# Keeping the source's order for eight more steps of a chunked recurrence with a feed-forward layer

## The chip, the core and the metric

One core of one Trainium2 chip. The metric is the device time of one execution in microseconds (us); times are compared as medians over runs. The engines named here are TensorE (PE, matrix products), VectorE (DVE), ScalarE (ACT), GpSimd (POOL) and SyncE (SP, which only issues DMAs here).

## What is computed

A gated linear recurrence over 4 batches of 8 heads of 768 positions, in chunks of 32, and behind it a feed-forward layer on its 3072 output rows of 256 values. Cut to what matters:

```python
for c in range(nc):                                   # 24 chunks of 32 positions
    L = np.exp(cum[:, :, :, None] - cum[:, :, None, :]) * causal
    M = np.einsum('bhin,bhjn->bhij', Cc, Bc) * L
    y_intra = np.einsum('bhij,bhjd->bhid', M, xc)
    y_inter = np.einsum('bhin,bhnd->bhid', Cc, state) * decay_to_i[:, :, :, None]
    y[:, :, sl] = y_intra + y_inter
    state = decay_full[:, :, None, None] * state + np.sum(Bx, axis=2)
h = y_rows @ w_in                                     # 256 -> 2048
g = np.maximum(h, 0.0) + np.log1p(np.exp(-np.abs(h))) # softplus
out = g @ w_out                                       # 2048 -> 256
```

## The kernel before

**Tiles.** The 768 positions are cut into six tiles u = 0 to 5 of 128 positions; with the four batches a tile holds 512 tokens. "Third tile" is u = 2, "fourth tile" u = 3. For each tile the recurrence makes a 256 x 512 input of the feed-forward layer, and this passes through 16 blocks k of 128 hidden units each.

**Words.** The source issues its work in words, one function each. For a tile u (and half p): `D` writes decays into `rm` (POOL, `affine_select`), `S` makes scores in PSUM (`sp`, PE), `M` multiplies these into `rm` (DVE), `B` scales B into `bp` and `C` scales C into `cc` (DVE), `T` scales the state into `td` (DVE), `U` (PE, `zp`), `I` and `R` (PE, `yp`) are products, `N` makes the next state `tb` (DVE), `G` multiplies `yp` into `gg` (DVE), `Xh` and `Xl` split the result into two parts `xh` (ACT) and `xl` (DVE). For a block k of tile j: `F` is the first product into `hp` (6 matmuls), `P` has three parts, `e` (softplus, ACT), `gh` (rounded copy, ACT, four buffers) and `gl` (the rest, DVE), and `Z` is the second product into `acc` (6 matmuls, which read `gh`, `gl`, `gh`, and again for the other half of the outputs).

**Order.** `ORDER` (lines 58 to 77) is a list of words written out by hand; it covers tiles 0, 1 and 2 of the recurrence and most blocks of the first two tiles. Its end, on which the case turns, is

```python
U2 P1.11 I2.1 R2 E0 G2.0 Z1.8 G2.1 N2 Z1.9 P1.11 P1.11 Xh2.0 Xl2.0 P1.12 P1.13 P1.13 Z1.10 Z1.11 Xh2.1 P1.12 P1.12
P1.15 P1.15 Xl2.1 P1.15
```

Behind it a loop runs over steps s from 32 (line 793). Step s issues Z of the block four steps back, then F and P of its own block, then the words that `FILLS` puts at this step. Steps 32 to 35 issue Z1.12 to Z1.15 and, at 35, `finish(1)`, which adds the sums of the second tile into `o` (two DVE operations) and stores them. Steps 32 to 47 hold F and P of the third tile's blocks 0 to 15; from step 36 their Z follow. For the fourth tile, `FILLS` gives: step 32, `D3.0` and loads for the next tile; step 37, `S3.0`, four `M3.0`, `D3.1`; step 39, `C3` (two operations), `B3.0`, `B3.1`, `T3`; step 40, `S3.1`, four `M3.1`; step 43, `U3 I3 R3 G3 Xh3 Xl3 N3`. The fifth and sixth tile have the same words 16 and 32 steps later.

**What sets the order on an engine.** PE and the DMA queue of SP are always kept in the source's order. DVE, ACT and POOL go through `InOrder` (lines 124 to 132): while `in_order[0]` is true each instruction is pinned behind everything that the source has issued on its engine before. From step `PINNED` on (lines 794 and 795) the flag is false, and the compiler's scheduler may place an instruction of these engines earlier than the source has it, wherever its inputs and buffers are ready in the scheduler's own simulation. The profile tells the two apart: a pinned instruction carries the wrapper's line, L131 (a load L140), a free one the line of its own function, as L400 for `B`, L410 for `C`, L438 for `T`, L396 for `M`, L356 for `D`, L611, L614 and L617 for the parts of `P`.

**Buffers that matter.** `bp` has two, `cc` and `td` one each, so the fourth tile's can be written once `U2`, `R2` and `N2` have read the third tile's. PSUM has six shared banks (`sp`, `hp`, `zp`, `yp`, `fp`) and two accumulators `acc`.

Of the kernel before, what the change touches and what calls it, by code (L numbers as in the profile page):

```python
# [76 lines left out]
"""  # L77
HALF = NFT // 2
AHEAD = 32
PINNED = 34  # L80
LAG = 4
WRAW = 4
END = 4
# [27 lines left out]
def recurrence_then_ffn(ctx: ExitStack, tc: tile.TileContext, un, alr, w_in, w_out, const, outT):  # L111
# [681 lines left out]
    for s in range(AHEAD, len(steps) + LAG):  # L793
        if s == PINNED:
            in_order[0] = False
# [54 lines left out]
```

## Time and profile before

| what | value |
|---|---|
| median of 3 runs | 319.69 us (318.64 to 319.97) |
| the profiled execution | 319.56 us |
| its span, first to last instruction | 317.9 us |
| PE busy | 307.7 us (97%) |
| ACT busy | 169.0 us (53%) |
| DVE busy | 160.9 us (51%) |
| POOL busy | 38.7 us (12%) |
| mean granted clock of TensorE | 0.995 |

Read it so: the profiled execution takes 1.66 us more than its span, and lies 0.13 us below the median. A granted clock of 1.00 is full speed (2.4 GHz), 0.50 the lower level (1.2 GHz). In the timelines an "x2" behind a row is a run of two instructions merged, and the brackets at its end are the idle time of the engine before it and what ended that.

### The profile page before, as it was taken

What the parts mean: (1) busy time and instruction counts of PE and PEld (TensorE: products, weight loads), DVE (VectorE), ACT (ScalarE), POOL (GpSimd) and SP (SyncE); (2) the same over time, 40 slices, a digit from 0 to 9 for tenths busy, and PEclk for the clock granted to TensorE, in tenths of its full rate; (3) what the DMA queues carried; (4) which work ended last, traced back from release to release, by engine and by line L of the source; (5) the groups of instructions that cost most, each with busy time, mean ns of one, the idle gap of its engine ahead of it and who ended that gap; (6) DMA issues with size and microseconds to landing.
All of it is one profiled execution on the core that took longest, in us unless ns stands there. A gap on an engine that the chain in (4) does not pass through costs nothing.

```text
span 317.9 us, 5610 instructions
## 1 busy us (share of the span) xinstructions
PE 307.7 (97%) x2308; PEld 252.9 (80%) x2308; DVE 160.9 (51%) x254; ACT 169.0 (53%) x290; POOL 38.7 (12%) x47
## 2 busy tenths in 40 slices
PE   4999999999999979999999999999999999999995
PEld 4877888888888858888888788888888888888885
DVE  3999995545544863345842345462354242322222
ACT  5799899696835244433344543444533444544450
POOL 5770800000000600000600000420000000000000
PEclk9999999999999979999999999999999999999999
DMA  7957947404000531100430100000100000100001
GB/s 225 405 219 222 381 161 198 134 0 165 2 0 0 193 108 35 64 3 0 150 117 2 66 2 0 3 0 2 66 1 2 3 0 0 64 4 0 2 0 66
DMA packets 10298, 24.37 MB, mean 77 GB/s; under 512 B 1056, under 2 KB 1696, under 8 KB 10272
## 3 DMA queue, kind: packets, MB, share of 16 engines
q1 hardware_dynamic: 10272, 24.01, 22.0%
q8 instruction: 18, 0.29, 0.4%
q14 instruction: 8, 0.07, 0.1%
HBM read 20.76 MB, written 3.24 MB: 76 GB/s over the span
## 4 chain that ended last, share of the span: by engine, by line
PE 92%; DVE 5%; DMA 1%; issue 1%; ACT 1%; DVEq 0%; ACTq 0%
PE acc L131 40%; PE hp L131 40%; PE sp L131 4%; PE yp L131 4%; DVE bp L400 1%; PE fp L131 1%; PE end L131 1%; DMA both_logs<-in_alr 1%; PE zp L131 1%; DVE rm L131 1%; DVE gg L131 0%; DVE wil L131 0%; DVE w L131 0%; PE gp L131 0%; DVE half L131 0%
## 5 line engine op out<-in xcount | busy, mean ns | idle before, releaser
L617 DVE TENSOR_TENSOR gl<-e,gh 128x512 fp32r<-128x512 f32 x62 | 42.9, 691 | 100.1 <-ACT gh L614 100.1
L611 ACT ACTIVATE e<-hp 128x512 f32<-128x512 f32 x62 | 37.1, 598 | 90.5 <-PE hp L131 90.1
L131 PE MATMUL hp<-xh,wih 128*128 128x512 f32 (+1 forms) x196 | 76.2, 389 | 0.5 <-DVE rm L131 0.5
L131 PE MATMUL acc<-gl,woh 128*128 128x512 f32 x188 | 74.1, 394 | 1.9 <-DVE gl L131 1.9
L131 PE MATMUL hp<-xl,wih 128*128 128x512 f32 (+1 forms) x196 | 75.5, 385 | 0.0
L131 PE MATMUL hp<-xh,wil 128*128 128x512 f32 (+1 forms) x196 | 75.5, 385 | 0.0
L131 PE MATMUL acc<-gh,woh 128*128 128x512 f32 x188 | 74.9, 398 | 0.0
L131 PE MATMUL acc<-gh,wol 128*128 128x512 f32 x188 | 73.9, 393 | 0.0
L131 PEld LDWEIGHTS hp<-xh,wih 128*128 128x128 f32 x196 | 37.0, 189 | 8.6 <-DVE rm L131 1.0
L131 PEld LDWEIGHTS acc<-gl,woh 128*128 128x128 f32 x188 | 35.5, 189 | 9.8 <-DVE gl L131 2.7
L131 PEld LDWEIGHTS hp<-xh,wil 128*128 128x128 f32 x196 | 36.8, 188 | 7.7 <-DVE wil L131 0.3
L131 PEld LDWEIGHTS hp<-xl,wih 128*128 128x128 f32 x196 | 36.9, 188 | 7.3
L131 PEld LDWEIGHTS acc<-gh,woh 128*128 128x128 f32 x188 | 35.6, 189 | 8.7 <-issue 0.9
L131 PEld LDWEIGHTS acc<-gh,wol 128*128 128x128 f32 x188 | 35.7, 190 | 7.4
L614 ACT CAST gh<-e 128x512 fp32r<-128x512 f32 x62 | 38.5, 621 | 5.1 <-PE acc L131 3.3
L131 DVE TENSOR_TENSOR gl<-e,gh 128x512 fp32r<-128x512 f32 x34 | 22.9, 688 | 22.1 <-ACT gh L131 22.1
L131 POOL TENSOR_SCALAR_AFFINE_SELECT rm<-fc 128x512 f32<-128x512 f32 (+1 forms) x25 | 22.9, 949 | 80.0 <-PE yp L131 76.2
L131 ACT CAST gh<-e 128x512 fp32r<-128x512 f32 x34 | 20.4, 617 | 10.8 <-PE acc L131 10.6
L131 ACT ACTIVATE e<-hp 128x512 f32<-128x512 f32 x34 | 19.7, 592 | 10.8 <-PE hp L131 7.2
L131 ACT ACTIVATE signs<-wraw 128x512 f16<-128x512 f32 (+1 forms) x32 | 24.2, 783 | 0.0
L356 POOL TENSOR_SCALAR_AFFINE_SELECT rm<-fc 128x2048 f32<-128x2048 f32 x5 | 13.0, 2624 | 87.9 <-PE yp L131 87.9
L131 DVE TENSOR_TENSOR rm<-sp,rm 128x512 f32<-128x512 f32 x24 | 15.5, 683 | 6.9 <-PE sp L131 6.6
(91 smaller groups left out, 222.5 us busy)
## 6 DMA issues: line engine op xcount, KB each, us to landing
un<-in_un SPq DMA_DIRECT2D x10, 768.0 KB, 6.2
wraw<-in_w_in SPq DMA_DIRECT2D x8, 512.0 KB, 5.4
wraw<-in_w_out SPq DMA_DIRECT2D x8, 512.0 KB, 4.3
gg<-gd SPq DMA_DIRECT2D x20, 128.0 KB, 3.4
out_t<-o SPq DMA_DIRECT2D x9, 256.0 KB, 2.1
head_in_h<-in_un SPq DMA_DIRECT2D x2, 384.0 KB, 5.1
head_in_l<-in_un SPq DMA_DIRECT2D x2, 384.0 KB, 6.6
out_t<-half SPq DMA_DIRECT2D x2, 256.0 KB, 2.2
```

What stands on the lines that cost most here:

```text
L131: return lambda *a, **k: tc.keep_in_program_order(f(*a, **k))
L356: Pl.affine_select(out=weights_of(u, p)[:, ks].rearrange("p h (c i) -> p (h c) i", i=SUB), in_=fs.rearrange("p h c -> p (h c)").unsqueeze( ...
L400: V.tensor_tensor(bp, home(u, p)[:, U_B:].rearrange("p (h n) -> p h n", n=N), f_tok[u][0][:, p * KP : (p + 1) * KP].unsqueeze(2).broadcast ...
L611: A.activation(e, h, AF.Softplus)
L614: A.copy(gh, e)
L617: V.tensor_tensor(gl, e, gh.bitcast(F32), op=ALU.subtract)
```

## The change

One constant is raised by eight.

```diff
 HALF = NFT // 2
 AHEAD = 32
-PINNED = 34
+PINNED = 42
 LAG = 4
```

So DVE, ACT and POOL keep the source's order through steps 34 to 41 as well; what the source issues from step 42 on stays free. Of the instructions in these eight steps, those on DVE are the `gl` of the third tile's blocks 2 to 9, `finish(1)`, `M3.0`, `C3`, `B3.0`, `B3.1`, `T3` and `M3.1`; those on ACT are the `e` and `gh` of the same blocks; the one on POOL is `D3.1`. No instruction is added, removed or resized.

## Rows read from the trace of the kernel before

**Rows 1.** Waits of PE, whole span: us in total, times, longest us

```profile
PE fp L131 <- ACT both_logs L131: 4.2, 1, 4.2
PE acc L131 <- DVE gl L131: 1.9, 1, 1.9
PE hp L131 <- DVE rm L131: 0.5, 1, 0.5
PE yp L131 <- DVE rm L131: 0.3, 1, 0.3
```

**Rows 2.** Windows, PE: length, busy time (instructions), granted clock, DMA share, GB/s

```profile
111.66:113.61 1.95, 0.00 (x1) 1.00 0.53 215
113.61:114.42 0.81, 0.81 (x4) 1.00 0.00 0
114.42:117.75 3.33, 3.33 (x9) 0.51 0.19 51
119.21:310.00 190.79, 190.79 (x1307) 1.00 0.07 24
```

**Rows 3.** Timeline of PE: start us, us, engine, line, operation, out<-in

```profile
106.03 1.10 PE L131 MATMUL yp<-cc,tb 32*64 32x128 f32 x32
...
108.33 0.39 PE L131 MATMUL acc<-gh,wol 128*128 128x512 f32 x1
...
109.69 0.39 PE L131 MATMUL acc<-gh,wol 128*128 128x512 f32 x1
...
111.05 0.39 PE L131 MATMUL acc<-gh,wol 128*128 128x512 f32 x1
111.27 0.39 PE L131 MATMUL acc<-gh,woh 128*128 128x512 f32 x1
...
117.75 0.47 PE L131 MATMUL hp<-xh,wih 128*128 128x512 f32 x1
...
128.73 0.39 PE L131 MATMUL acc<-gh,woh 128*128 128x512 f32 x1
```

**Rows 4.** Chain that ended last, in time: start us, us, what

```profile
106.40 3.83 DVE bp L400 x2
...
151.94 0.58 PE zp L131 x32
152.53 2.78 PE yp L131 x96
```

**Rows 5.** Timeline of DVE around the stall

```profile
107.64 2.59 DVE L400 TENSOR_TENSOR bp<-un,ft 128x256 f32<-128x256 f32 x1
...
112.88 0.68 DVE L131 TENSOR_TENSOR gl<-e,gh 128x512 fp32r<-128x512 f32 x1
...
125.53 1.37 DVE L681 TENSOR_TENSOR o<-acc,half 128x512 f32<-128x512 f32 x2 [1.43 <-PE acc L131]
```

**Rows 6.** Timeline of ACT

```profile
108.81 0.62 ACT L131 CAST gh<-e 128x512 fp32r<-128x512 f32 x1 [3.83 <-PE acc L131]
...
125.48 0.62 ACT L614 CAST gh<-e 128x512 fp32r<-128x512 f32 x1
```

**Rows 7.** Timeline of POOL

```profile
107.42 2.56 POOL L356 TENSOR_SCALAR_AFFINE_SELECT rm<-fc 128x2048 f32<-128x2048 f32 x1
153.55 5.47 POOL L356 TENSOR_SCALAR_AFFINE_SELECT rm<-fc 128x2048 f32<-128x2048 f32 x2 [43.58 <-PE yp L131]
```

**Rows 8.** Timeline of DVE later in the span

```profile
143.77 0.69 DVE L617 TENSOR_TENSOR gl<-e,gh 128x512 fp32r<-128x512 f32 x1 [2.02 <-ACT gh L614]
144.38 2.48 DVE L396 TENSOR_TENSOR rm<-sp,rm 128x512 f32<-128x512 f32 x4
...
153.23 0.41 DVE L400 TENSOR_TENSOR bp<-un,ft 128x256 f32<-128x256 f32 x1
...
154.16 2.60 DVE L438 TENSOR_TENSOR td<-tb,fr 128x256 f32<-128x256 f32 x1
156.69 1.27 DVE L517 TENSOR_TENSOR gg<-yp,gg 128x512 f32<-128x512 f32 x2
```

## Prediction

> **What bounds the kernel now.** I read the waits of PE first, because PE is busy for 307.7 of 317.9 us. There are four [rows 1]: 4.2 us at the start for the input, 0.5 and 0.3 for `rm`, and 1.9 us, once, for a `gl`. Only the last lies in the region that the change touches. The windows show where: PE does nothing from 111.66 to 113.61, runs at full clock for 0.81 us more, then 3.33 us at a granted clock of 0.51, the lower of the two levels; from 119.21 to 310 it is busy without a gap, at 1.00 [rows 2]. Two things follow. The stall costs more than its 1.95 us, since a slow stretch comes behind it. And whatever is won there goes straight to the end, because behind it PE never waits again until its last matmuls.
>
> The timeline of PE gives the whole loss. From the last matmul of Z1.8, at 108.33, to the last of Z1.9, at 109.69, are six, so one takes 1.36 / 6 = 0.227 us. Z1.11 begins at 111.27, and F2.0, which comes after twelve matmuls (Z1.11 and Z1.12), at 117.75 [rows 3]: 6.48 us where 12 x 0.227 = 2.72 would do. **3.76 us** are lost: 1.95 idle, 3.33 x (1 - 0.51) = 1.63 to the clock, and 0.18 where the pipe empties and fills.
>
> Why was that `gl` late? The chain of waits leads from `bp`, 3.83 us for two instructions of L400 [rows 4], to the `gl` of P1.11 at 112.88 [rows 5]. These are B3.0 and B3.1: words of step 39, free, which the scheduler has moved ahead of G2.0 at the end of the hand-written list. Behind them on DVE came `G2`, `N2`, and, also moved ahead, C3 and T3, and only then that `gl`. Its input was there much earlier: `gh` of P1.11 runs from 108.81 to 109.43 [rows 6].
>
> **The change part by part.**
>
> *The five operations leave.* All five words lie in steps 34 to 41, so they now stay behind what the source has ahead of them. DVE then goes on after `E0` with G2.0, which needs R2: 106.03 + 1.10 = 107.13 [rows 3]. The pair `gg` takes 1.27 [rows 8], to 108.4. For the two `tb` I take 0.41 each, the `bp` of [rows 8] with twice their columns: to 109.2. `gh` of P1.11 stays where it is, because it waits for the buffer that Z1.8 frees at 108.33 + 0.39 = 108.72 [rows 3, 6]. So its `gl` starts at 109.45 and is done at 110.14. The other bound: D3.1 holds POOL until 107.42 + 2.56 = 109.98 [rows 7], and beside it a `bp` that takes 0.41 alone took 2.59 and ended 0.25 us behind D3.1 [rows 5, 8]. If this `gl` has to wait out D3.1 as well, it ends at 109.98 + 0.69 = 110.67. PE wants it for the second matmul of Z1.11, at 111.27 + 0.23 = 111.50. Both bounds are early enough; this stall is gone.
>
> *What is late next.* Z1.12. Its `gh` needs the buffer that Z1.10 frees at 111.05 + 0.39 = 111.44; starting 0.09 later, as P1.11's did, it ends at 112.15; the `gl` runs from 112.18 to 112.87, and PE resumes 0.05 behind a `gl` (112.88 + 0.68 to 113.61 in the trace of before). PE would want it at 111.27 + 7 x 0.227 = 112.86 and gets it at 112.92: **0.06 us** of stall. Ahead of that `gh` ACT has five operations from 108.81 on. If none overlapped, at 0.62 each [rows 6], they would end at 111.91, and the stall would be 0.44. Operations in a row do overlap (a pair on DVE takes 1.27, not 2 x 0.69 [rows 8]), so I take 0.06 and keep 0.44 for the range.
>
> *The clock.* The fall to 0.51 comes 0.81 us after the only pause of this size, and the profile has no other fall behind the start: 190.79 us at 1.00 follow, with the same narrow products (`zp`, `yp`) inside [rows 2, 4]. I take it that without the pause there is no fall. The Trainium skill, page "TensorE: Matmul & The Clock Gate", section "HAM oscillation — how this bites in real kernels", asks for a longer pause than this one before the clock falls. By that rule the fall has another cause and stays, and 1.63 us of the gain would not come. The trace speaks against the rule here, with the fall right behind a pause of 1.95 us; it is the second rival.
>
> *The five operations arrive* at step 39, between `gl` of block 7 and of block 8. DVE is idle there for 2.02 us, until 143.77 [rows 8]; five at 0.41 take 2.05 at most. POOL is idle for 43.58 us ahead of 153.55 [rows 7], so the price of 2.59 does not apply. If it did, they would take up to 5 x 2.60 = 13 us, as the `td` beside POOL [rows 8] (last rival). M3.1 follows from 144.38 to 146.86; PE wants its result for I3.1, behind I3.0 in the products that start at 152.53 [rows 4], and `bp` for U3 at 151.94: more than 5 us of slack hide them. Cost: nothing.
>
> *`finish(1)`* now stays behind the `gl` of block 2, ahead of which it ran at 125.53 [rows 5]. That `gl` follows its `gh`, 125.48 + 0.62, and ends at 126.8; the pair then at 126.8 + 1.37 = 128.2. Z2.0, which overwrites the sums it reads, starts at 128.73 [rows 3], so 0.5 us is left. Its stores go out some 1.3 us later on SP; the source's next transfer on that queue is at step 48, so nothing is held up.
>
> *The rest* (`gl`, M3.0, M3.1, and `e` and `gh` on ACT) has its inputs from PE, in PE's order, and already ran in the source's order. D3.1 has only D3.0 ahead of it on POOL and stays at 107.42. Cost: nothing.
>
> **Sum.** 3.76 - 0.06 = 3.70 us, between 3.32 and 3.76. Of the profiled execution's 319.56 that leaves 315.9. That execution lies 0.13 below the median; 319.69 - 3.70 = **316.0**. With the spread of the runs, from 318.64 - 3.76 = 314.9 to 319.97 - 3.32 = 316.7.
>
> **The rivals.**
>
> *The clock falls all the same.* The narrow products of U2, I2 and R2 lie ahead of it, too. Then 1.63 us stay lost: 319.69 - 2.07 = 317.6. Against it: the same products ran at 151.94 to 155.3 with no fall [rows 2, 4].
>
> *POOL takes the place of the moved work.* `gg` and `tb` now run beside D3.1. If it held `gg` as it held `bp`, G2.0 would end at 110.2, the pair at 110.8, `tb` at 111.6, the `gl` at 112.3: 0.85 us of stall instead of 1.95, hence 316.8, or 318.5 if the clock falls too. Against it: a `gg` pair took its plain 1.27 beside a POOL stretch of 153.55 to 159.02, in which `td` took 2.60 [rows 7, 8].
>
> *The change does not do what it says.* Words from step 42 on are still free. B4 and C4 of step 55 could fill the gap as B3 and C3 did, at the same price, and the time stays at 319.7. For it: that is how the stall came about. Against it: they need the buffers of `bp` and `cc` that B3 and C3 have first claim to, and that only U3 and R3 empty; in the trace of before the next `bp` runs behind `zp` at 151.94 [rows 4, 8].
>
> *Slower: the five pile up at step 39.* With 13 us instead of 2 they would end at 154.8, and the `gl` and M3.1 behind them at 157.9. PE would stall for M3.1 at 153.5 for 4.4 us, and lose 1.63 to the clock: 316.0 + 6.0 = 322.0. PE begins to wait once they take over 8.6 us, and the kernel is slower than before by over 1.6 us only from 12.3 on. Against it: this needs a busy POOL, and POOL is idle there.
>
> **How the numbers follow.** The forecast has 0.80, the clock 0.07, POOL 0.05, no effect 0.05, the pile 0.03. The forecast's own span, 314.9 to 316.7, holds less than 8 in 10 once a stray median is allowed for, so the range reaches over the clock's case: 314.9 to 317.7. Half a per cent, 1.6 us, is about what a measurement of this kernel can tell from no change. Faster by more: 0.80 + 0.07 + about half of POOL's 0.05 = 0.89. Within: 0.05 + 0.03 = 0.08. Slower: 0.03.
>
> **What would show it.** Right: the wait of PE for `gl` is gone from the list or under 0.5 us, the granted clock is 1.00 from 15 us on, F2.0 starts near 114.0, and five DVE operations of some 0.41 us, all with L131, lie between two `gl` near 138 to 140. `gl` of P1.11 well past 111.5 would show POOL in the way; a clock near 0.5 with no pause ahead of it, the second case; `bp` or `cc` of the fifth tile ahead of 115, the third; a wait for `rm` near 150, the last. The prediction is wrong if PE finds another late `gl` between Z1.11 and F2.0 that I took for early.

## The result: 316.29 us, 1.05% less

| | before | after |
|---|---|---|
| median of 4 runs | 319.81 us (318.64 to 319.97) | 316.29 us (315.66 to 316.49) |
| ratio of the means, 95% interval | | 0.9895 [0.9867, 0.9922] |
| span of the profiled execution | 317.9 us | 314.7 us |
| mean granted clock of that execution | 0.995 | 1.000 |

The kernel before has runs in which TensorE's clock falls behind the pause and runs in which it does not, about 1 us apart (experiment 4), and three of its four runs here, and the profiled one, lie where the clock fell.

The waits of PE in the kernel after (total, times, longest, in us):

```profile
PE fp L131 <- ACT both_logs L131: 4.2, 1, 4.2
PE hp L131 <- DVE rm L131: 0.7, 2, 0.5
PE yp L131 <- DVE rm L131: 0.3, 1, 0.3
```

The 1.9 us for a `gl` in [rows 1] is gone, and nothing of its size has come in its place. The windows of PE (length, busy, granted clock, DMA share, GB/s), from the start of Z1.11 to F2.0 and from there to the end of the dense part:

```profile
111.81:114.73 2.92, 2.92 (x13) 1.00 0.61 253
114.73:306.00 191.27, 191.27 (x1309) 1.00 0.08 26
```

Where [rows 2] had a pause of 1.95 us and 3.33 us at 0.51, there are now 2.92 us at full clock. The timeline of PE, which answers to [rows 3]:

```profile
106.57 1.10 PE L131 MATMUL yp<-cc,tb 32*64 32x128 f32 x32
...
111.81 0.39 PE L131 MATMUL acc<-gh,woh 128*128 128x512 f32 x1
...
113.17 0.39 PE L131 MATMUL acc<-gh,woh 128*128 128x512 f32 x1
113.47 0.50 PE L131 MATMUL acc<-gl,woh 128*128 128x512 f32 x1
113.81 0.40 PE L131 MATMUL acc<-gh,wol 128*128 128x512 f32 x1
...
114.73 0.39 PE L131 MATMUL hp<-xh,wih 128*128 128x512 f32 x1
...
125.61 0.39 PE L131 MATMUL acc<-gh,woh 128*128 128x512 f32 x1
```

From Z1.11's first matmul (111.81) to F2.0's (114.73) it takes 2.92 us; before it took 117.75 - 111.27 = 6.48. So this place gained **3.56 us**. The spans differ by only 3.2, because this execution reached R2 0.54 us later than that of before (106.57 against 106.03), for a reason that has nothing to do with the change (last section), and was 0.18 us quicker behind F2.0: 3.56 - 0.54 + 0.18 = 3.20.

The timeline of DVE, first around the old stall, then where the five operations have gone:

```profile
107.71 1.29 DVE L131 TENSOR_TENSOR gg<-yp,gg 128x512 f32<-128x512 f32 x2 [0.76 <-PE yp L131]
108.91 0.60 DVE L131 SCALAR_TENSOR_TENSOR tb<-zp,kb,td 128x128 f32<-128x128 f32 x2
110.00 0.87 DVE L131 TENSOR_TENSOR gl<-e,gh 128x512 fp32r<-128x512 f32 x1 [0.49 <-ACT gh L131]
...
112.72 0.69 DVE L131 TENSOR_TENSOR gl<-e,gh 128x512 fp32r<-128x512 f32 x1 [0.50 <-ACT gh L131]
...
123.63 1.28 DVE L131 TENSOR_TENSOR o<-acc,half 128x512 f32<-128x512 f32 x2
...
138.55 0.76 DVE L131 TENSOR_TENSOR cc<-un,fr 128x256 f32<-128x256 f32 x2
139.22 0.76 DVE L131 TENSOR_TENSOR bp<-un,ft 128x256 f32<-128x256 f32 x2
139.89 0.42 DVE L131 TENSOR_TENSOR td<-tb,fr 128x256 f32<-128x256 f32 x1
140.66 0.69 DVE L131 TENSOR_TENSOR gl<-e,gh 128x512 fp32r<-128x512 f32 x1 [0.35 <-ACT gh L131]
```

and POOL and ACT in the same stretch (POOL's two selects merged):

```profile
105.47 4.88 POOL L131 TENSOR_SCALAR_AFFINE_SELECT rm<-fc 128x2048 f32<-128x2048 f32 x2 [66.78 <-PE yp L131]
```

```profile
109.35 0.62 ACT L131 CAST gh<-e 128x512 fp32r<-128x512 f32 x1 [3.83 <-PE acc L131]
...
112.07 0.62 ACT L131 CAST gh<-e 128x512 fp32r<-128x512 f32 x1
```

All five carry L131 now. They stand between the `gl` of blocks 7 and 8, take 1.76 us from 138.55 to 140.31, and the `gl` behind them still waits 0.35 us for its own `gh`: they fit into idle time. The `bp` pair takes 0.76 us where it took 3.83 [rows 4].

### The profile page after: what moved, and what is told of

It reads as the page before. It is cut to its first block, busy times and chain, and to the rows that moved or that the text cites. A ratio compares the mean times of both kernels' runs of the same rounds, so it can differ in the third digit from the quotient of the medians.

```text
span 314.7 us, 5611 instructions
## 1 busy us (share of the span) xinstructions
PE 306.2 (97%) x2308; PEld 251.6 (80%) x2308; DVE 158.8 (50%) x254; ACT 168.9 (54%) x290; POOL 38.4 (12%) x47
## 4 chain that ended last, share of the span: by engine, by line
PE 95%; DVE 2%; DMA 1%; issue 1%; ACT 0%; DVEq 0%
PE acc L131 41%; PE hp L131 40%; PE yp L131 5%; PE sp L131 5%; PE fp L131 1%; PE end L131 1%; PE zp L131 1%; DVE rm L131 1%; DMA both_logs<-in_alr 1%; DVE wil L131 0%; DVE w L131 0%; PE gp L131 0%; DVE xl L131 0%; DVE bp L131 0%; ACT xh L131 0%
## 5 line engine op out<-in xcount | busy, mean ns | idle before, releaser
L617 DVE TENSOR_TENSOR gl<-e,gh 128x512 fp32r<-128x512 f32 x54 | 37.3, 692 | 88.8 <-ACT gh L614 88.7
L131 PE MATMUL hp<-xh,wih 128*128 128x512 f32 (+1 forms) x196 | 76.3, 389 | 0.7 <-DVE rm L131 0.7
L131 PE MATMUL hp<-xl,wih 128*128 128x512 f32 (+1 forms) x196 | 75.6, 386 | 0.0
L131 PE MATMUL hp<-xh,wil 128*128 128x512 f32 (+1 forms) x196 | 75.5, 385 | 0.0
L131 PE MATMUL acc<-gh,woh 128*128 128x512 f32 x188 | 74.4, 396 | 0.0
L131 PE MATMUL acc<-gl,woh 128*128 128x512 f32 x188 | 73.5, 391 | 0.0
L131 PE MATMUL acc<-gh,wol 128*128 128x512 f32 x188 | 73.2, 389 | 0.0
L131 DVE TENSOR_TENSOR gl<-e,gh 128x512 fp32r<-128x512 f32 x42 | 29.3, 708 | 33.2 <-ACT gh L131 33.0
L131 PEld LDWEIGHTS hp<-xh,wih 128*128 128x128 f32 x196 | 36.8, 188 | 9.1 <-DVE rm L131 1.6
L131 PEld LDWEIGHTS hp<-xh,wil 128*128 128x128 f32 x196 | 36.8, 188 | 7.7 <-DVE wil L131 0.3
L131 PEld LDWEIGHTS hp<-xl,wih 128*128 128x128 f32 x196 | 36.8, 188 | 7.2
L131 PEld LDWEIGHTS acc<-gh,woh 128*128 128x128 f32 x188 | 35.3, 188 | 8.6 <-issue 0.9
L131 PEld LDWEIGHTS acc<-gl,woh 128*128 128x128 f32 x188 | 35.3, 188 | 7.4 <-DVE gl L131 0.3
L131 PEld LDWEIGHTS acc<-gh,wol 128*128 128x128 f32 x188 | 35.3, 188 | 7.3
L131 ACT ACTIVATE e<-hp 128x512 f32<-128x512 f32 x42 | 24.6, 594 | 23.5 <-PE hp L131 19.7
L131 POOL TENSOR_SCALAR_AFFINE_SELECT rm<-fc 128x512 f32<-128x512 f32 (+1 forms) x26 | 25.1, 1000 | 80.7 <-PE yp L131 76.8
L131 ACT CAST gh<-e 128x512 fp32r<-128x512 f32 x42 | 25.3, 617 | 10.9 <-PE acc L131 10.4
L131 ACT ACTIVATE signs<-wraw 128x512 f16<-128x512 f32 (+1 forms) x32 | 24.2, 785 | 0.0
L131 DVE TENSOR_TENSOR rm<-sp,rm 128x512 f32<-128x512 f32 x32 | 20.4, 683 | 6.9 <-PE sp L131 6.6
L356 POOL TENSOR_SCALAR_AFFINE_SELECT rm<-fc 128x2048 f32<-128x2048 f32 x4 | 10.5, 2640 | 84.4 <-PE yp L131 84.4
```

The source lines that it names most:

```text
L131: return lambda *a, **k: tc.keep_in_program_order(f(*a, **k))
L356: Pl.affine_select(out=weights_of(u, p)[:, ks].rearrange("p h (c i) -> p (h c) i", i=SUB), in_=fs.rearrange("p h c -> p (h c)").unsqueeze( ...
L617: V.tensor_tensor(gl, e, gh.bitcast(F32), op=ALU.subtract)
```

## The experiments

Ratios are to the kernel before, run beside each group on the same chip; its median was 318.63 us in the group of `e3`, `e4`, `e8` and `e9` and 319.38 to 319.54 in the others, as more or fewer of its runs had the fall of the clock, so versions are best compared by their own times. Five questions: is it these five operations, why were they dear, does each count alike, what made the clock fall, and does running ahead cost anywhere else.

**1. The five words alone, and all but the five.** `e1` leaves `PINNED` at 34 and pins only these words:

```diff
         for word in fills[s]:
+            held = in_order[0]
+            in_order[0] = held or word in ("C3", "B3.0", "B3.1", "T3")
             act(word)
+            in_order[0] = held
```

> PINNED stays at 34; only C3, B3.0, B3.1 and T3 are pinned, so the five DVE operations go back behind the gl of block 7 and nothing else moves. Theory (the five ahead of the gl of P1.11 are the whole cost): 316.3 us, PE's 1.9 us wait gone, clock 1.00 throughout. Rival (the kept order of the other instructions of steps 34 to 41, finish(1) above all, gives the gain): 319.8.

Measured: 316.39 us, 0.9906 [0.9882, 0.9930], clock 1.00. `e2` has `PINNED = 42` with `held and word not in (...)`, so everything but the five is pinned.

> PINNED is 42, but C3, B3.0, B3.1 and T3 are left free, so only the rest of the change is made. Theory: 319.8 us, the wait of 1.9 us and the slow clock behind it as before. Rival (the other instructions give the gain): 316.3.

Measured: 318.81 us, 0.9992 [0.9975, 1.001], a microsecond less than I gave: in seven of its ten runs the clock stayed at 1.00 (318.38 to 319.22 us), in three it fell (319.55 to 320.47), as it does in some runs of before and not in others. The profiled execution is one of the three, and its wait and its slow stretch are those of [rows 1, 2]:

```profile
PE acc L131 <- DVE gl L131: 2.0, 1, 2.0
...
112.25:114.20 1.95, 0.00 (x1) 1.00 0.61 253
114.20:115.50 1.30, 1.30 (x6) 1.00 0.00 0
115.50:118.50 3.00, 2.85 (x8) 0.54 0.21 72
```

So the five operations are the whole effect; the order of `finish(1)` and the rest is worth nothing that these runs can tell.

**2. Why they were dear.** `e6` keeps the order of before and takes POOL away from the place. Its selects must wait for two one-column memsets, pinned on DVE behind the `gl` of step 32:

```diff
         for word in fills[s]:
+            if word == "D3.0":
+                for p in range(NP):
+                    V.memset(weights_of(3, p)[:, :1, :1], 0.0)
             act(word)
```

> The order of before, but D3.0 and D3.1 are made to wait on POOL: two one-column memsets of the two rm buffers are pinned on DVE behind the gl of step 32, so POOL is idle from 105 to about 118 us. The five operations stay ahead of the gl of P1.11, and the load of the fifth tile's inputs still runs beside them. Theory (POOL's reads make bp slow, the operations themselves are cheap): bp 0.41 us each instead of 1.3 and 2.6, gl of P1.11 done near 110.9, no wait of PE over 0.3 us, 316.4 us. Rival 1 (the load of un, which runs at the same time, makes bp slow): bp as before, 319.8. Rival 2 (five operations ahead of the gl are too many at any price): bp quick, but a wait of PE of 1 us or more and 317.5 or over.

Measured: 316.35 us, 0.9910 [0.9880, 0.9940]. DVE and POOL:

```profile
106.83 0.75 DVE L400 TENSOR_TENSOR bp<-un,ft 128x256 f32<-128x256 f32 x2
...
110.40 0.69 DVE L131 TENSOR_TENSOR gl<-e,gh 128x512 fp32r<-128x512 f32 x1
...
118.43 2.40 POOL L131 TENSOR_SCALAR_AFFINE_SELECT rm<-fc 128x2048 f32<-128x2048 f32 x1 [79.77 <-DVE rm L131]
```

The five still run ahead of the `gl` of P1.11, as L400 shows, the load of `un` still runs beside them (the DMA engines are 85% busy from 106.8 to 110.4 us), and the whole gain is there. The order as such cost nothing: the cost was that `bp` met D3.0 and D3.1. The Trainium skill, page "SBUF — State Buffer", section "Who interferes with whom", says that a DVE operation with two inputs in SBUF and a GpSimd operation that reads SBUF exclude each other, and whichever starts first keeps the other out until it is done. The rows agree: 0.41 us alone, 2.59 beside D3.1 [rows 5, 8], and `gg`, with one of its inputs in PSUM, at its plain price beside POOL.

**3. Does each of the five count alike?** `e5` pins B3 alone (`FILLS` names B ahead of C), `e4` pins C3 and T3 alone (T behind C), each with the lines of `e1` and its own words.

> PINNED is 34; B3.0 and B3.1 alone are pinned behind the gl of block 7 (FILLS names B ahead of C, so that the pin holds); C3 and T3 stay free and ahead of the gl of P1.11. Theory: gg and tb end near 109.0 to 109.5, the first cc waits out D3.1 to about 110.2 to 110.8, the second and td take 0.33 each, gl of P1.11 ends near 111.6 to 112.2, so PE waits 0.1 to 0.6 us; 316.4 to 317.0 without a fall of the clock. Rival (C3 and T3 cost as much as B3): a wait of 1 us or more and 318 or over.

Measured: 316.14 us, 0.9902 [0.9880, 0.9924], less than the 316.4 to 317.0 that I gave:

```profile
108.98 1.52 DVE L410 TENSOR_TENSOR cc<-un,fr 128x256 f32<-128x256 f32 x2
...
113.30 0.50 PE L131 MATMUL acc<-gl,woh 128*128 128x512 f32 x1 [0.17 <-DVE gl L131]
```

With B back in its place, C3 and T3 may run ahead for nothing: PE waits 0.17 us, and the time is that of `e1`.

> PINNED is 34; C3 and T3 are pinned behind the gl of block 7 (FILLS names T behind C), B3.0 and B3.1 stay free and ahead of G2.0, beside D3.1. Theory (the two bp bear the cost): bp 1.3 and 2.6 us as before, gl of P1.11 0.7 to 1.0 us earlier than before, a wait of PE of about 1.0 us. Then 317.0 to 317.4 if the clock holds through a pause of that size, 318.6 to 319.0 if it falls. Rival (the number of operations ahead counts, not their price beside POOL): a wait of 0.3 us or less and 316.5.

Measured: 317.44 us, 0.9958 [0.9942, 0.9974]:

```profile
106.82 3.92 DVE L400 TENSOR_TENSOR bp<-un,ft 128x256 f32<-128x256 f32 x2
...
112.16:113.10 0.94, 0.00 (x0) 1.00 0.97 405
113.10:120.00 6.90, 6.75 (x28) 1.00 0.31 97
```

B3 alone costs 317.44 - 316.39 = 1.05 us, C3 and T3 alone nothing, all five 2.2 where the clock holds (318.59, experiment 4) and 3.2 where it falls (319.61). The parts do not add up: with B in front, C3 and T3 lengthen the pause from 0.94 to 1.95 us, and behind the longer one the clock falls in about half of the runs, where it fell in none of the ten of `e4`. `e3` keeps all five ahead and only puts B behind C (C3 free, B pinned behind it):

> PINNED is 34; B3.0 and B3.1 are pinned behind C3, which stays free: all five operations are still ahead of the gl of P1.11, but in the order cc, cc, bp, bp, td and behind gg and tb, so only the first cc starts while D3.1 runs. Theory (each price is set by what POOL does when the operation starts): cc 1.5 us for the pair, bp 0.41 each, a wait of PE of 0.5 to 0.9 us, 316.8 to 317.2 with the clock at 1.00. Rival (bp is slow of itself): bp over 0.8 us each and a wait as before, 319.4.

Measured: 317.07 us, 0.9951 [0.9930, 0.9972].

```profile
108.77 1.52 DVE L410 TENSOR_TENSOR cc<-un,fr 128x256 f32<-128x256 f32 x2
110.20 0.75 DVE L131 TENSOR_TENSOR bp<-un,ft 128x256 f32<-128x256 f32 x2
...
111.94 0.50 PE L131 MATMUL acc<-gl,woh 128*128 128x512 f32 x1 [0.40 <-DVE gl L131]
```

The wait is 0.40 us where I gave 0.5 to 0.9. `bp` costs 0.41 once D3.1 is over: the price hangs on what POOL does when the operation starts, not on the operation.

**4. What brings the clock down?** Here the kernel after gets a pause of its own making, with the five operations away: memsets of a scratch tile on DVE ahead of the `gl` of P1.11, ten in `e8`, seven in `e9`, then five in `e11` and six in `e12`.

```diff
-N2 Z1.9 P1.11 P1.11 Xh2.0 ...
+N2 Z1.9 X10 P1.11 P1.11 Xh2.0 ...
+    def hold_vector(n):
+        idle = cp.tile([P, 512], F32, name="idle")
+        for _ in range(n):
+            V.memset(idle, 0.0)
```

> The kernel after the change, with ten 128x512 memsets of a scratch tile on DVE ahead of the gl of P1.11, so that PE pauses there for 1.5 to 2.2 us as it did before, with bp, cc and td away. Theory (the pause alone brings the clock down): a stretch of some 3 us at 0.5 behind the pause and 319.2 to 319.8 us. Rival (the fall had another cause, as a page of the Trainium skill would have it): the clock stays at 1.00 and only the pause is added, 317.8 to 318.4.

> The same with seven memsets: a pause of 0.4 to 1.0 us. Theory (a pause this short leaves the clock alone): 316.8 to 317.3 us. Rival (any pause at this place brings it down): 318.4 to 318.9.

Both pauses came out longer than planned, since a memset into the same tile waits for the one ahead of it (row in the last section): one each 0.66 us, where the planned pauses go with some 0.41. `e8`: 322.84 us, 1.0125 [1.0098, 1.0152]; `e9`: 319.94 us, 1.0032 [1.0016, 1.0049]. Their windows of PE, `e8` first:

```profile
112.07:116.44 4.37, 0.00 (x0) 0.80 0.24 102
116.44:121.30 4.86, 4.86 (x12) 0.50 0.18 62
```

```profile
111.58:113.98 2.40, 0.00 (x0) 1.00 0.44 180
113.98:114.70 0.72, 0.72 (x2) 0.73 0.00 0
114.70:117.70 3.00, 3.00 (x8) 0.50 0.09 27
```

A pause without the five operations is followed by the same slow stretch; in `e8` the clock falls within the pause already (0.80 over its 4.37 us). So `e9`, meant as the short pause, became a second long one. The short ones:

> The kernel after with five memsets instead of seven. One takes 0.66 us in a row with the others, so the pause is 2.40 - 2 x 0.66 = 1.1 us, about that of the kernel with B alone ahead (0.94), which had no fall of the clock. Theory (a pause this short leaves the clock alone): 1.00 throughout, 317.4 to 317.9 us. Rival (there the clock held for another reason, not for the shorter pause): a stretch at 0.5 and 318.9 or more.

> The same with six memsets, a pause of 2.40 - 0.66 = 1.74 us, just under the 1.95 of the kernel before. Theory (the pause, not what caused it, decides): either it holds and gives 318.0 to 318.5, or it falls and gives 319.3 to 319.9; nothing between, unless the fall is shorter than before.

Measured: 317.45 us, 0.9938 [0.9924, 0.9953], and 318.12 us, 0.9979 [0.9958, 1.0]. The waits of PE in the two, and a window of the second:

```profile
PE acc L131 <- DVE gl L131: 1.1, 1, 1.1
```

```profile
PE acc L131 <- DVE gl L131: 1.7, 1, 1.7
...
113.50:120.00 6.50, 6.36 (x27) 1.00 0.20 65
```

The clock held at 1.00 in both profiled executions. Each run has its mean granted clock on record, and a fall shows in it: 3.33 us at 0.51 make 0.995 of a whole run, and without one it reads 0.998 to 1.000.

| pause of PE in the profiled execution | kernel | runs with the fall |
|---|---|---|
| none or under 0.5 us | after, `e1`, `e3`, `e5`, `e6`, `e7`, `e10` | 0 of 29 |
| 0.94 us | `e4` | 0 of 10 |
| 1.08 us | `e11` | 0 of 8 |
| 1.74 us | `e12` | 1 of 8 |
| 1.95 us | before | 30 of 58 |
| 1.95 us | `e2` | 3 of 10 |
| 2.40 us | `e9` | 8 of 8 |
| 4.37 us | `e8` | 4 of 4 (0.989) |

So it is the pause, and not `bp`, that the fall needs. The narrow products ahead of it (`zp`, `yp`) stand in all these kernels: without a pause they bring no fall, but whether they have a part in it is not shown. Nor is it shown what decides at 1.95 us.

What does a fall cost? The 28 runs of before at 1.00 take 318.30 to 319.28 us, median 318.59; the 30 at 0.995 take 319.28 to 320.31, median 319.61. That is 1.02 us, less than the 1.63 of the slow stretch. `e12`, whose profiled execution paused for 1.74 us and kept its clock, shows where the rest may go:

```profile
111.19 0.39 PE L131 MATMUL acc<-gh,woh 128*128 128x512 f32 x1
...
114.59 0.40 PE L131 MATMUL acc<-gh,woh 128*128 128x512 f32 x1
115.12 0.50 PE L131 MATMUL acc<-gl,woh 128*128 128x512 f32 x1
...
116.39 0.39 PE L131 MATMUL hp<-xh,wih 128*128 128x512 f32 x1
```

From Z1.11 to F2.0 it takes 5.20 us and loses 5.20 - 2.72 = 2.48. The execution of before lost 3.76 with a pause 0.21 longer, so the fall itself cost it 3.76 - 2.48 - 0.21 = 1.07. At full clock PE is quicker at the `gl` of Z1.12 and stops there a second time (0.53 us between two starts instead of 0.227), which the slow stretch hides.

**5. Running ahead elsewhere, and a rival for the best time.** `e7` sets `PINNED = 1000`, so nothing runs ahead to the end.

> The flag never falls: DVE, ACT and POOL keep the source's order to the end, for the fifth and sixth tile too, where cc, bp and td still run ahead in the kernel after (a td of 2.60 us beside POOL at 151 us). Theory (running ahead costs only where PE is near a wait; those two places have several us of slack): 316.3 us, within 0.3 of the kernel after. Rival (what runs ahead there also costs): 315.5 or less.

Measured: 316.00 us (315.85 to 316.17), 0.9898 [0.9872, 0.9923]: no difference from after that these runs can tell. One thing moved there: the pair `xl` of the fourth tile now meets POOL,

```profile
153.19 2.97 DVE L131 TENSOR_TENSOR xl<-gg,xh 128x512 fp32r<-128x512 f32 x2
```

and nobody waits for it. `e10` is about a meeting in the early part, told in the last section:

```diff
-un2.0 W6 W3 W3 P0.5 w12 S2.0 M2.0.0 un2.1
+un2.0 W6 W3 P0.5 w12 S2.0 M2.0.0 W3 un2.1
```

> The kernel after the change, with M2.0.0 moved on DVE ahead of the weight's or-operation W3 (its fourth part) at 36 to 38 us. In some executions the gl at 34.6 us starts before a POOL select and takes 0.69, in others behind it and takes 1.26, and then the first M2.0 and PE's next product are 0.5 us later. Theory (that meeting of DVE and POOL is most of the spread between executions): PE's second wait for rm gone in either case, the runs closer together, 315.7 to 316.1 us. Rival (the weight part that is now later holds PE instead): a wait for wol or woh near 40 us and 316.3 or more.

Measured: 316.29 us (316.17 to 316.43), 0.9907 [0.9888, 0.9926]. The second wait for `rm` is not in the list, but the profiled execution is one in which the meeting went well anyway. The spread is small, 0.26 us, but that of `e5`, which lacks this change, is 0.21. What the rival asks for is there: PE's weight load waits for the `wol` that now comes later,

```profile
40.17 0.19 PEld L131 LDWEIGHTS acc<-gh,wol 128*128 128x128 f32 x1 [0.37 <-DVE wol L131]
```

and then for a `gl` behind it, and the twelve matmuls from 39.61 us take 3.13 us instead of 2.72. So the order costs 0.4 us there in this execution; whether the meeting makes most of the spread is not settled. No version here beats the kernel after by more than the runs differ.

## Why the prediction was right

- **The loss and its place.** 3.76 us between Z1.11 and F2.0, all from five operations on DVE: shown by `e1` and `e2`. Measured gain at the place, between the two profiled executions: 3.56.
- **The `gl` of P1.11.** Given as done between 110.14 and 110.67 on the clock of before, which is 110.68 to 111.21 on that of after (0.54 later). It ran from 110.00 to 110.87: it met the end of D3.1 and lost 0.18 us, between the bounds, and PE wanted it at 112.04.
- **The next late one.** Z1.12's `gl` it was, and the chain came out as worked out: `gh` at 112.07, which is 0.09 behind Z1.10's end, `gl` done at 113.41, PE at 113.47. The term was mis-sized all the same: 0.06 forecast, 0.20 measured (2.92 - 2.72). The wait itself is 0.07 (0.30 between two starts instead of 0.227); the matmul behind the restarted one comes 0.34 later instead of 0.227, and that refill of the pipe, which I had counted as part of the old loss, stands at a small wait too.
- **The clock.** That it would not fall without the pause is shown, and that the pause was the cause, too (`e8`, `e9`). The page "TensorE: Matmul & The Clock Gate" of the Trainium skill, section "HAM oscillation — how this bites in real kernels", asks for a longer pause; here 1.95 and 2.40 us were enough, so the measurement decides against it. What the prediction did not see is that the fall is not in every run: the kernel before has it in 30 of 58. It took 1.63 us as the price, which is right as a part of the 3.76 that the profiled execution lost, but against a run without a fall the price is 1.02 by the medians and 1.07 by the rows of `e12`.
- **The arrival.** Price 0.41 each and no delay: 1.76 us for the five, and a `gl` behind them that waits for its input, as forecast. `finish(1)`: done at 124.91, Z2.0 at 125.61, 0.7 us left where I had 0.5.
- **POOL in the way of `gg` and `tb`.** It was not: 1.29 and 0.60 us for the pairs beside D3.1.
- **The sum.** 316.0 forecast, 316.29 measured. Of the 0.3 too much, 0.14 is the term of Z1.12; the rest is less than the runs differ by. One piece of luck is in it: the profiled execution and the median from which the 3.70 was taken both had the fall. From a median like the 318.63 of one group of runs the same sum would have given 314.9. Against the runs of before that keep their clock (318.59) the change gains 2.30 us, against the others (319.61) 3.32.

Nor did the prediction see how unequal the five are. It gave `bp` the blame for the late `gl` and counted `cc` and `td` along; `e4` and `e5` show that B alone would have cost 1.05 us and C and T alone nothing, and that C and T cost a microsecond and more once B is in front of them.

## What to carry to other kernels

Where a scheduler may move work ahead, look in the trace for the first thing that PE waits for and ask what was put in front of it; a line that tells free from pinned instructions makes that one look. Ask of a slow instruction what ran on the other engine beside it before changing the order: here taking POOL away from the place gave the same 3 us as putting the order right. And a pause of PE has two prices, its own length and, behind the longer ones here, a slow stretch, so the last part of a pause can cost more than its length: `e12` took 318.12 us with 1.74 us of pause, `e9` 319.94 with 2.40. Where that stretch comes in some runs and not in others, look at the granted clock of each run before taking a median for the time of the kernel.

## What was not expected of the hardware

**A meeting of DVE and POOL that goes either way.** At 34.6 us a `gl` with both inputs in SBUF starts within a row of eight selects on POOL. Before and after run the same instructions there; first the `gl` of before and the select beside it, then those of after:

```profile
34.57 0.69 DVE L131 TENSOR_TENSOR gl<-e,gh 128x512 fp32r<-128x512 f32 x1 [0.33 <-ACT gh L131]
34.59 1.26 POOL L131 TENSOR_SCALAR_AFFINE_SELECT rm<-fc 128x512 f32<-128x512 f32 x1
```

```profile
34.62 1.26 DVE L131 TENSOR_TENSOR gl<-e,gh 128x512 fp32r<-128x512 f32 x1 [0.31 <-ACT gh L131]
34.64 0.72 POOL L131 TENSOR_SCALAR_AFFINE_SELECT rm<-fc 128x512 f32<-128x512 f32 x1
```

One of the two runs at its plain price (0.69 or 0.72 us) and the other is held up to 1.26. In the 14 profiled executions the `gl` took 0.69 or 0.70 eight times and 1.26 six times. Where it took 1.26, R2 began between 106.44 and 106.62 us; where it took 0.69, between 105.91 and 106.16 (106.33 in `e10`, whose order differs). Half a microsecond of the difference between two executions thus goes with which of the two is held up, and two profiles must be compared from the same place on, not by their spans. What decides it is not shown: by the rows the `gl` starts 0.02 us ahead of the select in both.

**Memsets that wait for themselves.** 128x512 memsets on DVE into the same tile start 0.66 us apart, with 0.17 us idle ahead of each that the row (of `e9`) puts down to the one before, where two independent 128x512 operations start 0.60 to 0.61 apart though each lasts longer (0.69 against 0.48).

```profile
109.60 0.48 DVE L131 MEMSET idle<- 128x512 f32 x1 [0.17 <-DVE idle L131]
```
